# An attention and mixture-of-experts kernel: slot 0's list from one-hots of 168 places, and the gate's reciprocal taken in the expert slots

## The chip, the cores and the metric

The kernel runs on one core of one Trainium2 chip. The metric is the device time of one execution in microseconds (us); of the kernel before three executions were timed. The engines are TensorE (PE, with its weight loads as PEld), VectorE (DVE), ScalarE (ACT), GpSimd (POOL) and SyncE (SP, which here only issues transfers). ACT and POOL issue transfers too. Each engine runs its own fixed queue of instructions from first to last, and queues meet only at semaphores.

## The reference

Three layers run one behind the other: a causal attention (2 batches, 8 heads, 576 rows, 64 wide), then two mixtures of 8 experts over the 1152 rows of 512 that it leaves. What matters here is the first mixture:

```python
logits = x @ w_gate
expert_idx = np.argmax(logits, axis=1)
logits_s = logits - logits.max(-1, keepdims=True)
probs = np.exp(logits_s)
probs /= probs.sum(-1, keepdims=True) + 1e-09
gate_w = probs[np.arange(N), expert_idx]
for i in range(N):
    e = expert_idx[i]
    if counts[e] < capacity:
        disp[e, counts[e]] = x[i]; pos[i] = counts[e]; counts[e] += 1; keep[i] = True
h = np.maximum(np.einsum('ecd,edf->ecf', disp, w1), 0.0)
y = np.einsum('ecf,efd->ecd', h, w2)
for i in range(N):
    if keep[i]:
        out[i] = gate_w[i] * y[expert_idx[i], pos[i]]
```

The chosen expert's logit less the maximum is zero, so the gate is 1 / (sum of the exponentials + 1e-9). The second mixture is alike, with a bias by modality on the logits and no capacity.

## The kernel before

**Attention** goes by pairs of heads, four per batch. Its rows are written to a table x1 in HBM, 528 columns wide: 512 of the row, then column GATE (the gate), the token's number and the second mixture's biases. Rows lie on 128 partitions in NT = 5 tiles per batch.

**The door** is what this text calls the stretch between the last attention product and the first expert product, 97 to 109 us. For batch 1 `route` there takes the logits' maximum, the one-hot of the chosen expert (`oh1`), and by PE the counts of earlier rows with the same choice (`pr`); the exponentials' sum is taken by `gates`, which adds 1e-9, takes the reciprocal and puts it into x1's rows in SBUF (`xrow`, column GATE). Then four transfers write the last columns of batch 1 to x1 (`keep_rows`; the last one goes out on ACT's queue, row L268, the one before it on SP's, L269). Meanwhile `place` turns ranks into one-hots: a row's rank in its expert is split into a place inside a column of H1 = 96 (`here`, `lpos`) and the number of the column (`lcol` for all experts' columns, `lcol0` for the two columns of expert 0). PE multiplies them into lists of row numbers by `listing`: `pl0`, copied to `list0`, the rows of expert 0; and `pli`, copied to `list1`, those of all. Between these products, and behind them, PE runs products that nobody reads, to stay busy (`awake`; AWAKE gives their number at four places, the third of which, 14, stands right before slot 0's transposes).

**The slots.** Expert 0 is slot 0. Its rows come by two gathers of POOL (L828, reading x1 by `list0`) into the tile xc; PE transposes them (`ptx`, L869), ACT copies them (`xn`), and 128 products (L905) follow, first 64 into `ps`, in four groups j = 0 to 3 of 16. The PSUM pool of `ps` has two buffers, so group j = 2 can start only when both halves of group 0 have been read, one by ACT (L977) and one by DVE (L979, which is ordered behind ACT's). The experts after it run in an order of falling counts, `perm`, which DVE works out behind the lists (`key` to `perm`, L1206 to L1216). SP loads `perm` to know which expert's weights to fetch (L1122, then L146), POOL loads it to know which part of `list1` slot 1 gathers (L1118, then L1131 and L828). After a slot's first product come its tail's steps in `tail1`: the second mixture's logits, scaled by the row's gate, and its own gate times the first one's.

**What sets the order.** The order on each engine is made when the program is built, from the order of the code, pinned instructions (`keep_in_program_order`, `issue_after`) and a scheduler; `tail1`'s code before its first `yield` is in the program at the slot's beginning. On the chip each queue then runs as it stands.

Of the kernel before, what the change touches and what calls it, by code (L numbers as in the profile page):

```python
# [25 lines left out]
WHOLE = 72  # L26
RW = 528
# [19 lines left out]
AWAKE = 15, 6, 14, 4  # L47
# [7 lines left out]
def shape_constants():  # L55
# [9 lines left out]
    t = {"io8": np.broadcast_to(e - E, (NT, E)), "tok": tok, "tok1": tok1, "col": np.arange(E * J2),  # L65
# [27 lines left out]
def build(tc, ctx, spots, tab, qk, v, s, wg, wa, cap, mod, wg2, mb, wb, out):  # L93
# [42 lines left out]
    lcol0 = [ac.tile([P, NT, W1], F32R, name=f"lcol0{b}") for b in range(B)]  # L136
# [22 lines left out]
    def place(m, ge, rank, keep, pos, colm, num, p, nt, pool, colm0=None, rest=None, plain=None):  # L159
# [17 lines left out]
        def onehots():  # L177
            if keep is not None:
                here = pool.tile([p, shared, hc], F32R, name="here", bufs=1)
                shape = [p, shared, hc]  # L180
                order_ = []
                if plain is not None:
                    two = [p, nt, W[m]]
                    nc.vector.tensor_tensor(colm0, col[:p, 0:W[m]].unsqueeze(1).to_broadcast(two),
                                            hj.unsqueeze(2).to_broadcast(two), op=ALU.is_equal)
                    two = [p, shared, W[m]]
                    order_.append(nc.vector.tensor_tensor(colm0[:, 0:shared], colm0[:, 0:shared].bitcast(F32),
                                                          num[:, 0:shared].unsqueeze(2).to_broadcast(two),
                                                          op=ALU.mult).ins)
                    plain.append(here)  # L190
                with tc.issue_after(order_[0]) if order_ else ExitStack():
                    order_[1:] = [nc.vector.tensor_tensor(here, col[:p, 0:hc].unsqueeze(1).to_broadcast(shape),
                                            pb_[:, 0:shared].unsqueeze(2).to_broadcast(shape), op=ALU.is_equal).ins]
                for t in range(shared):
                    nc.scalar.mul(pos[:, t, :], here[:, t, :].bitcast(F32), num[:, t:t + 1])
            for t in range(shared, nt):
                with tc.issue_after(order_[-1]) if plain is not None else ExitStack():
                    last = nc.vector.tensor_scalar(pos[:, t, :], col[:p, 0:hc], pb_[:, t:t + 1], num[:, t:t + 1],
                                                   op0=ALU.is_equal, op1=ALU.mult)
            if colm0 is not None and plain is None:  # L200
# [3 lines left out]
            with tc.issue_after(last.ins):  # L204
                for t0, t1 in parts:
                    shape = [p, t1 - t0, 8 * nj]
                    def columns(t0=t0, t1=t1, shape=shape):
                        return nc.vector.tensor_tensor(colm[:, t0:t1],
                                                       col[:p, 0:8 * nj].unsqueeze(1).to_broadcast(shape),
                                                       hj[:, t0:t1].unsqueeze(2).to_broadcast(shape), op=ALU.is_equal)  # L210
                    if plain is not None and t0 == 0:
                        plain.append(columns)
                    else:
                        last = columns()
# [12 lines left out]
    with ExitStack() as actx:  # L227
# [44 lines left out]
        def route(b, behind_=None):  # L272
# [38 lines left out]
            nc.vector.tensor_tensor(rk, pr, oh1[b], op=ALU.mult)  # L311
# [4 lines left out]
            placing = lambda rest=None, plain=None: place(1, ge, rank, capf, lpos[b], lcol[b], tok1[:, b, :], P, NT, ap,  # L316
                                                          lcol0[b], rest, plain)
            if b:
                placing(plain=plain)
# [4 lines left out]
        postponed, plain = [], []  # L324
# [212 lines left out]
        def values(k):  # L537
# [15 lines left out]
            nc.vector.tensor_copy(k.xu[:, 320:576], pb)  # L553
# [56 lines left out]
        for n in range(2 * 2 * 4 + 1):  # L610
# [55 lines left out]
            if n == 7:  # L666
# [3 lines left out]
                with tc.issue_after(operands[-1]):  # L670
                    nc.gpsimd.tensor_copy(capf, capi[:, 0:1])
                    nc.gpsimd.tensor_copy(modf, modi[:, :, :, 0])
                for bb in range(B):
# [11 lines left out]
        with tc.issue_after(moved[0]):  # L685
            postponed.pop()()
# [14 lines left out]
        with tc.issue_after(counted.ins):  # L701
            awake(filler, ones, wide, AWAKE[1])
        pl0 = pst.tile([H1, W1], F32, tag="t", name="pl0")
        by_engine = [[0, 1, 2, 3, 4], [3, 4, 0, 1, 2]]
        in_line = [by_engine[0], by_engine[0]]

        def listing(dst, lc, b, between=False, turns=by_engine):
            for t in turns[b]:
                spot = plain[0] if b and t < 3 and turns is in_line else lpos[b]
                ins = nc.tensor.matmul(dst, spot[:, t, :], lc[b][:, t, :], start=(b == 0 and t == 0),  # L710
                                       stop=(b == 1 and t == turns[1][-1])).ins
# [788 lines left out]
```

## Time and profile before

| what | us |
|---|---|
| median of three executions | 391.19 |
| their lowest and highest | 391.06, 391.35 |
| the profiled execution's own time | 390.84 |
| its span | 389.1 |

The span is the time between the first and the last instruction of the profiled execution; 1.7 us of its time lie around it. Mean granted TensorE clock over the span is 0.988 of full speed. PE is busy for 97% of the span, DVE for 51%, ACT for 45%, POOL for 33%. Such shares are averages: the door is a small part of the span, and it is read from the timeline of each engine there. In a timeline row the first number is the start, the second the time that the row covers (several like instructions are one row, with their count behind the x), and in brackets stands the idle time before it and what released it.

### The profile page before, as it was taken

The page shows a single profiled execution, that of the slowest core. Times are in us where ns is not written, and L with a number is a line of the kernel's source. Part 1 is how long each engine was busy: PE and PEld are TensorE (multiplying, and loading weights), DVE is VectorE, ACT ScalarE, POOL GpSimd, SP SyncE. Part 2 cuts the span into 40 slices and gives each one's busy share as a digit, 9 for nine tenths or more (in the row PEclk, how much of TensorE's full clock was granted, in tenths as well). Part 3 has the DMA queues.
Part 4 walks back from the last instruction along what each step waited for, and adds up shares of the span by engine and source line. Part 5 has one row for each costly group of instructions (what it writes and reads, how often), then busy time and mean ns, then how long its engine had stood idle before and what let it go on. Part 6 is the DMA issues. An engine that isn't in the chain of part 4 may idle for free.

```text
span 389.1 us, 8687 instructions
## 1 busy us (share of the span) xinstructions
PE 376.5 (97%) x3058; PEld 353.6 (91%) x3058; DVE 198.6 (51%) x801; ACT 175.9 (45%) x473; POOL 126.8 (33%) x178
## 2 busy tenths in 40 slices
PE   7899999999999999999999999999999999999993
PEld 3788888888689999999999999999999999999992
DVE  6878889888826764251515161569722444221110
ACT  7999999996325632121221122155233464131120
POOL 4777877650270040421202002000425265020020
PEclk9699999999999999999999999999999999999998
DMA  5864699912159963969798779861287457010010
GB/s 189 289 196 161 238 373 380 322 72 93 55 177 290 353 192 95 322 201 320 234 319 236 258 210 291 280 217 36 61 310 292 123 168 219 5 39 21 0 56 25
DMA packets 29782, 75.08 MB, mean 193 GB/s; under 512 B 7547, under 2 KB 10859, under 8 KB 29728
## 3 DMA queue, kind: packets, MB, share of 16 engines
q1 hardware_dynamic: 27020, 67.19, 51.9%
q0 software_dynamic: 2624, 7.19, 6.4%
q8 instruction: 26, 0.43, 0.5%
q14 instruction: 28, 0.23, 0.2%
q10 hardware_dynamic: 84, 0.04, 0.0%
HBM read 63.97 MB, written 11.07 MB: 193 GB/s over the span
## 4 chain that ended last, share of the span: by engine, by line
PE 77%; issue 7%; DMA 6%; DVE 3%; POOL 3%; ACT 1%; SPq 1%; POOLq 1%; DVEq 0%; ACTq 0%
PE ps L905 30%; PE ps L913 7%; PE ps L914 7%; PE ps L915 7%; PE pt L423 5%; PE ps L423 4%; DMA qkd<-in_qk 4%; PE ps L909 3%; PE pb L423 2%; PE ptx L869 2%; PE pa L423 2%; DMA out<-yo,oi 2%; PE px L423 2%; PE pty L1001 1%; PE ps L911 1%
## 5 line engine op out<-in xcount | busy, mean ns | idle before, releaser
L905 PE MATMUL ps<-xn,st 128*128 128x160 f32 (+6 forms) x512 | 70.1, 290 | 0.3 <-ACT xn L890 0.3
L905 PEld LDWEIGHTS ps<-xn,st 128*128 128x128 f32 x512 | 66.2, 190 | 0.6 <-ACT xn L890 0.4
L905 PE MATMUL ps<-hidden,st 128*128 128x160 f32 (+5 forms) x448 | 62.4, 293 | 0.0
L905 PEld LDWEIGHTS ps<-hidden,st 128*128 128x128 f32 x448 | 58.5, 190 | 0.0
L513 ACT ACTIVATE e<-sc,nmx 128x192 f32<-128x192 f32 (+4 forms) x80 | 44.7, 561 | 1.6 <-DVE nmx L504 1.4
L971 DVE COPY yT<-ps 128x276 f32<-128x276 f32 (+6 forms) x22 | 8.0, 362 | 70.0 <-ACT yT L970 70.0
L913 PE MATMUL ps<-xs,hi 128*128 128x276 f32 x128 | 38.4, 300 | 0.0
L913 PE MATMUL ps<-hidden,hi 128*128 128x276 f32 x128 | 38.1, 298 | 0.0
L914 PE MATMUL ps<-xs,hi 128*128 128x276 f32 x128 | 37.1, 290 | 0.0
L915 PE MATMUL ps<-xs,lo 128*128 128x276 f32 x128 | 37.1, 290 | 0.0
L915 PE MATMUL ps<-hidden,lo 128*128 128x276 f32 x128 | 37.1, 290 | 0.0
L914 PE MATMUL ps<-hidden,hi 128*128 128x276 f32 x128 | 37.1, 290 | 0.0
L423 PE MATMUL pt<-ident,e 128*128 128x128 f32 x224 | 35.1, 288 | 0.5 <-ACT xu L552 0.4
L970 ACT COPY yT<-ps 128x276 f32<-128x276 f32 (+6 forms) x22 | 7.1, 323 | 60.6 <-PE ps L905 33.2
L423 PE MATMUL ps<-ka,qa 128*128 128x320 f32 (+2 forms) x96 | 31.0, 337 | 2.6 <-DVE nmx L504 1.4
L1092 POOL DMA_INDIRECT out<-yo,oi x13 | 12.4, 954 | 54.5 <-ACT yo L992 44.9
L803 DVE TENSOR_TENSOR lo<-st,hi 128x512 fp32r<-128x512 f32 x40 | 28.3, 730 | 1.1 <-ACT hi L801 1.0
L801 ACT CAST hi<-st 128x512 fp32r<-128x512 f32 x48 | 27.5, 620 | 0.0
L423 PEld LDWEIGHTS pt<-ident,e 128*128 128x128 f32 x224 | 25.9, 146 | 1.5 <-ACT xu L552 0.5
L828 POOL DMA_INDIRECT xc<-x,idx x14 | 13.9, 995 | 40.8 <-PE pr L1055 23.4
L984 DVE SCALAR_TENSOR_TENSOR hidden<-ps,hidden 128x552 fp32r<-128x552 f32 x16 | 11.7, 732 | 28.3 <-ACT hidden L982 28.2
L504 DVE CUSTOM_DVE_ANT_0 sc<-ps,later 128x192 f32<-128x192 f32 (+1 forms) x64 | 24.5, 413 | 2.7 <-PE ps L423 1.6
(317 smaller groups left out, 832.1 us busy)
## 6 DMA issues: line engine op xcount, KB each, us to landing
st<-in_wa SPq DMA_DIRECT2D x64, 512.0 KB
st<-in_wb SPq DMA_DIRECT2D x24, 512.0 KB
qkd<-in_qk SPq DMA_DIRECT2D x6, 1152.0 KB
vt<-in_v SPq DMA_DIRECT2D x8, 320.0 KB
qkd<-in_qk SPq DMA_DIRECT2D x4, 576.0 KB
out<-zrow SPq DMA_DIRECT2D x1, 2304.0 KB
y<-yt SPq DMA_DIRECT2D x8, 256.0 KB
x<-xrow SPq DMA_DIRECT2D x2, 768.0 KB
```

Of the source, the lines that this page charges most:

```text
L423: ins = op(*args, **kw)
L504: least[:] = [nc.vector.tensor_tensor_reduce(h.sc[t][:r, c0:c1], ps[:r, o0:o0 + c1 - c0], later[:r, m0:m0 + c1 - c0], -0.125, low, op0=ALU ...
L513: recent[:] = [nc.scalar.activation(to, h.sc[t][:r, :w], AF.Exp, bias=h.nmx[t][:r], scale=-1.0, accum_out=rsum[:r, k.b, t, n:n + 1]).ins]
L801: nc.scalar.copy(hi[:, c:c + h], st[:, c:c + h])
L803: eng.tensor_tensor(lo[:, c:c + h], st[:, c:c + h], hi[:, c:c + h].bitcast(F32), op=ALU.subtract)
L828: nc.gpsimd.indirect_dma_start(out=k.xc[:r, i, 0:rw], out_offset=None, in_=src, in_offset=bass.IndirectOffsetOnAxis(ap=idx[:r, i:i + 1], a ...
L905: pin(nc.tensor.matmul(out[:, 0:c], w[:, o:o + P], mv, start=first, stop=last, skip_group_check=True))
L913: pin(nc.tensor.matmul(out[:, 0:c], hi, mv[:, 0, :], start=first, stop=False, skip_group_check=True))
L914: pin(nc.tensor.matmul(out[:, 0:c], hi, mv[:, 1, :], start=False, stop=False, skip_group_check=True))
L915: pin(nc.tensor.matmul(out[:, 0:c], lo, mv[:, 0, :], start=False, stop=last, skip_group_check=True))
L984: fence(relu, nc.vector.scalar_tensor_tensor(k.hs[:, 2 * j:2 * j + 2, 1, :], k.b, 0.0, hi.bitcast(F32), op0=ALU.max, op1=ALU.subtract))
L1092: put = nc.gpsimd.indirect_dma_start(out=out, out_offset=bass.IndirectOffsetOnAxis(ap=oi[:, i:i + 1], axis=0), in_=yr[:, i, :], in_offset= ...
```

## The change

Slot 0's list for batch 1 no longer comes from places in a column times columns. For expert 0 the row's place in 168 is its count in `pr` itself, so DVE makes `r0` (the count, or a number out of range where another expert was chosen) and compares it with the numbers 0 to 167 (`col0`, made earlier on POOL, with places beyond the capacity moved out of range): `spots0`, in two instructions of 3 and 2 tiles. Ten products of one column pair each (`spots0` half by half, against a tile `tokr` with the token in one of two columns) add to `pl0`. The rest of `place` for batch 1 follows behind. `gates` only sums, straight into x1's column GATE; the 1e-9 and the reciprocal move to the beginning of `tail1`, once per slot, into `g1`, which the later steps read. AWAKE's second number falls from 6 to 3. The core of the diff:

```diff
+WHERE = 96 + WHOLE
-AWAKE = 15, 6, 14, 4
+AWAKE = 15, 3, 14, 4
             def gates():
-                g = ap.tile([P, NT], F32, name="g")
-                nc.vector.tensor_reduce(g, ex, axis=AX.X, op=ALU.add)
-                nc.vector.tensor_scalar_add(g, g, 1.0e-9)
-                return nc.vector.reciprocal(xrow[:, :, GATE], g).ins
+                return nc.vector.tensor_reduce(xrow[:, :, GATE], ex, axis=AX.X, op=ALU.add).ins
...
+            if b:
+                r0 = ap.tile([P, NT], F32, name="r0")
+                nc.vector.scalar_tensor_tensor(r0, oh1[1][:, :, 0], NONE, pr[:, :, 0], op0=ALU.mult, op1=ALU.add)
+                for t0, t1 in ((0, 3), (3, NT)):
+                    shape = [P, t1 - t0, WHERE]
+                    chosen = nc.vector.tensor_tensor(spots0[:, t0:t1, 0:WHERE], col0.unsqueeze(1).to_broadcast(shape),
+                                                     r0[:, t0:t1].unsqueeze(2).to_broadcast(shape), op=ALU.is_equal)
...
+                    nc.gpsimd.memset(tokr.bitcast(F32), 0.0)
+                    nc.gpsimd.memset(spots0[:, :, WHERE:C1].bitcast(F32), 0.0)
+                    nc.gpsimd.tensor_copy(tokr[:, :, 1], tok1[:, 1, :])
+                    nc.gpsimd.tensor_scalar(col0, col[:, 0:WHERE], capf, NONE, op0=ALU.is_ge, op1=ALU.mult)
...
-        first_list = listing(pl0, lcol0, 1, True, in_line)
+        for t in range(NT):
+            for i in (1, 0):
+                with tc.issue_after(ins):
+                    ins = nc.tensor.matmul(pl0, spots0[:, t, H1 * i:H1 * i + H1], tokr[:, t, 1 - i:3 - i], start=False,
+                                           stop=t == NT - 1 and i == 0).ins
         list0 = const.tile([H1, W1], I32, name="list0")
-        with tc.issue_after(listed(list0, pl0, 1).ins):
-            plain[1]()
-        with tc.issue_after(first_list):
-            placed = listing(pli, lcol, 1, True)
+        listed(list0, pl0, 1)
+        with tc.issue_after(ins):
+            placed = listing(pli, lcol[1], 1, [3, 4, 0, 1, 2], True)
...
     def tail1(k, c):
 
         k.yr, l8 = yrs[c % 2], l8s[c % 2]
+        g1 = mp.tile([H1, 2], F32, name="g1")
+        nc.vector.tensor_scalar_add(g1, k.xc[:, :, GATE], 1.0e-9)
+        nc.vector.reciprocal(g1, g1)
...
-            nc.vector.scalar_tensor_tensor(lg[:, i], lg[:, i], k.xc[:, i, GATE:GATE + 1], k.xc[:, i, BIAS:BIAS + E],
+            nc.vector.scalar_tensor_tensor(lg[:, i], lg[:, i], g1[:, i:i + 1], k.xc[:, i, BIAS:BIAS + E],
...
-        nc.vector.tensor_tensor(k.yr[:, :, GATE - DM], g, k.xc[:, :, GATE], op=ALU.mult)
+        nc.vector.tensor_tensor(k.yr[:, :, GATE - DM], g, g1, op=ALU.mult)
```

Three places in the queues move. On DVE, where the door's one-hots and lists are made, before (a name's number tells apart tiles of one name; 86 and 88 are batch 1's, 90 is `lcol0`'s; `list_1859` is `list0`):

```order
L174 SCALAR_TENSOR_TENSOR kept<-rank,capf,ctab 128x5
L166 TENSOR_REDUCE pb__1792<-ge 128x5
L168 TENSOR_REDUCE hj<-ge 128x5
L169 SCALAR_TENSOR_TENSOR pb__1792<-pb__1792,rank 128x5
L184 TENSOR_TENSOR lcol_90<-ctab,hj 128x10
L187 TENSOR_TENSOR lcol_90<-lcol_90,kept 128x6
L192 TENSOR_TENSOR here<-ctab,pb__1792 128x288
L198 TENSOR_SCALAR lpos_86<-ctab,pb__1792,kept 128x96 x2
L208 TENSOR_TENSOR lcol_88<-ctab,hj 128x208
L224 TENSOR_SCALAR list_1859<-pl_1839 96x2
L208 TENSOR_TENSOR lcol_88<-ctab,hj 128x312
```

After, first the new one-hots, and then the rest from `kept` on (`list_1862` is `list0`):

```order
L295 SCALAR_TENSOR_TENSOR r_1789<-oh_1_84,pr 128x5
L696 TENSOR_REDUCE cnt_1834<-pcnt 128x8
L298 TENSOR_TENSOR spots_90<-col_91,r_1789 128x3x168
L298 TENSOR_TENSOR spots_90<-col_91,r_1789 128x2x168
L302 TENSOR_TENSOR rk<-pr,oh_1_84 128x40
```

```order
L178 SCALAR_TENSOR_TENSOR kept<-rank,capf,ctab 128x5
L210 TENSOR_SCALAR list_1862<-pl_1841 96x2
L170 TENSOR_REDUCE pb__1798<-ge 128x5
L172 TENSOR_REDUCE hj<-ge 128x5
L173 SCALAR_TENSOR_TENSOR pb__1798<-pb__1798,rank 128x5
L185 TENSOR_TENSOR here<-ctab,pb__1798 128x288
L190 TENSOR_SCALAR lpos_86<-ctab,pb__1798,kept 128x96 x2
L199 TENSOR_TENSOR lcol_88<-ctab,hj 128x312
L199 TENSOR_TENSOR lcol_88<-ctab,hj 128x208
```

`spots0` and `list0` now stand ahead of `here`, `lpos` and both `lcol`, and of the two `lcol` the one of 208 elements, tiles 3 and 4, has become the last.

On PE, the products of the lists of batch 1 before (`pl_1839` is `pl0`, `pli` has the names 86 and 88 in it; L714 are the fillers between, L156 the first of the 14):

```order
L710 MATMUL pl_1839<-lcol_90,lpos_86 96x2
L710 MATMUL pli<-lcol_88,lpos_86 96x104
L714 LDWEIGHTS ones
L714 MATMUL ps<-ones 128x128
L710 MATMUL pli<-lcol_88,lpos_86 96x104
L714 LDWEIGHTS ones
L714 MATMUL ps<-ones 128x128
```

and after, from batch 0's products on:

```order
L705 MATMUL pli<-lcol_87,lpos_85 96x104 x5
L725 MATMUL pl_1841<-tokr,spots_90 96x2 x10
L705 MATMUL pli<-lcol_88,lpos_86 96x104
L709 LDWEIGHTS ones
L709 MATMUL ps<-ones 128x128
L705 MATMUL pli<-lcol_88,lpos_86 96x104
```

The five products of `pl0` with fillers between have become ten without; `pli`'s products, which start with tile 3, and then the 14 fillers follow as before.

On DVE behind the lists, before, around `perm` and then, eight rows on, ahead of `hidden` (`inv` belongs to slots 0 and 1, `hidden` to slot 0's first products):

```order
L1228 TENSOR_REDUCE wid<-eqw 128x7
L1216 TENSOR_TENSOR perm<-key,ctab 128x14
L1230 TENSOR_TENSOR more<-cnt_1829,wid 128x8
L1231 TENSOR_TENSOR more<-more,cnt_1829 128x8
L761 TENSOR_TENSOR s1cc<-more,ctab 128x48
L1010 TENSOR_SCALAR inv<-idx 96x2
```

```order
L774 TENSOR_TENSOR s1to<-s1ge,s1nxt 128x7x7
L778 TENSOR_REDUCE s1res<-s1ge 128x7
L777 TENSOR_REDUCE s1res<-s1to 128x7
L979 TENSOR_SCALAR hidden_1915<-ps 128x160 x3
L803 TENSOR_TENSOR lo<-st,hi 128x512
```

and after (`g_2198` is slot 0's `g1` from its rows `xc_710`, `g_2516` slot 1's from `xc_712`):

```order
L1229 TENSOR_REDUCE wid<-eqw 128x7
L1015 TENSOR_SCALAR g_2198<-xc_710 96x2
L1217 TENSOR_TENSOR perm<-key,ctab 128x14
L1231 TENSOR_TENSOR more<-cnt_1834,wid 128x8
L1016 RECIPROCAL g_2198<-g_2198 96x2
```

and, further on,

```order
L776 TENSOR_REDUCE s1res<-s1ge 128x7
L775 TENSOR_REDUCE s1res<-s1to 128x7
L1015 TENSOR_SCALAR g_2516<-xc_712 96x2
L1016 RECIPROCAL g_2516<-g_2516 96x2
L977 TENSOR_SCALAR hidden_1917<-ps 128x160 x3
L801 TENSOR_TENSOR lo<-st,hi 128x512
```

An instruction that reads slot 0's gathered rows now stands right ahead of `perm`, and two that read slot 1's stand right ahead of `hidden`.

## Rows read from the trace of the kernel before

**Rows 1.** By stretch: us, busy PE, PEld, DVE, ACT, POOL; PEclk, DMA, GB/s
```profile
97.00:104.00 7.00, 6.14 (x58) 4.69 (x57) 6.19 (x36) 3.30 (x14) 0.00 (x0) 1.00 0.16 47
109.00:127.00 18.00, 18.00 (x136) 18.00 (x137) 8.03 (x18) 6.93 (x18) 7.54 (x16) 1.00 0.81 259
350.00:373.00 23.00, 23.00 (x191) 23.00 (x190) 3.09 (x8) 4.16 (x10) 1.84 (x2) 1.00 0.04 12
```
**Rows 2.** Timeline (start us, us, what) of PE: fillers, transposes, slot 0's products
```profile
104.18 3.19 PE L156 MATMUL ps<-ones 128*128 128x512 bf16 x14
108.13 0.47 PE L869 MATMUL ptx<-ident,xc 72*128 72x72 f32 x4 [0.21 <-DMA xc<-x,list]
108.90 8.96 PE L905 MATMUL ps<-xn,st 128*128 128x160 f32 x64 [0.30 <-ACT xn L890]
```
**Rows 3.** POOL's queue at L828 (ns min/median/max, first, last start), then timeline
```profile
L828 POOLq EVENT_SEMAPHORE  x3: 43/43/214, 102.9 to 103.3; - x3
104.10 0.98 POOL L828 DMA_INDIRECT xc<-x,list  x1 [18.85 <-DVE s1to L773]
105.39 0.97 POOL L828 DMA_INDIRECT xc<-x,list  x1 [0.30 <-DVE wid L1228]
```
**Rows 4.** Timeline of the door, the last writes of x1 and their sources
```profile
99.49 0.50 ACT L589 ACTIVATE xrow<-ps,rinv 128x64 f32<-128x64 f32 x2
100.12 0.19 DVE L305 RECIPROCAL xrow<-g 128x5 f32<-128x5 f32 x1
100.48 0.51 ACTq L268 DMA_DIRECT2D x<-xrow  x1
```
**Rows 5.** Timeline of DVE, one-hots and lists of the door
```profile
100.37 0.20 DVE L311 TENSOR_TENSOR rk<-pr,oh 128x40 f32<-128x40 f32 x1
101.79 0.45 DVE L192 TENSOR_TENSOR here<-ctab,pb__1792 128x288 fp32r<-128x288 f32 x1
102.16 0.56 DVE L198 TENSOR_SCALAR lpos<-ctab,pb__1792,kept 128x96 fp32r<-128x96 f32 x2
102.64 0.37 DVE L208 TENSOR_TENSOR lcol<-ctab,hj 128x208 fp32r<-128x208 f32 x1
103.09 0.16 DVE L224 TENSOR_SCALAR list<-pl 96x2 int32<-96x2 f32 x1
103.17 0.47 DVE L208 TENSOR_TENSOR lcol<-ctab,hj 128x312 fp32r<-128x312 f32 x1
103.82 0.17 DVE L1206 SCALAR_TENSOR_TENSOR key<-cnt,ctab 128x7 f32<-128x7 f32 x1 [0.19 <-DVE lcol L208]
```
**Rows 6.** Timeline, `perm`, POOL's load of it and slot 1's gathers
```profile
105.28 0.17 DVE L1216 TENSOR_TENSOR perm<-key,ctab 128x14 int32<-128x14 f32 x1
L1118 POOLq TENSOR_LOAD <-perm x1: 498/498/498, 107.1 to 107.1; - x1
108.90 1.01 POOL L828 DMA_INDIRECT xc<-x,idx  x1 [0.59 <-POOL idx L1131]
110.22 0.96 POOL L828 DMA_INDIRECT xc<-x,idx  x1 [0.31 <-issue]
```
**Rows 7.** Transfers of the stretch 88 to 112, median us from issue to landing
```profile
xc<-x,list POOLq DMA_INDIRECT x2, 2.9
xc<-x,idx POOLq DMA_INDIRECT x2, 3.3
```
**Rows 8.** Waits of the same stretch (us in total, times, longest); then `hidden` on DVE
```profile
DVE inv L1010 <- POOL idx L1131: 2.1, 2, 1.2
111.77 0.32 DVE L979 TENSOR_SCALAR hidden<-ps 128x160 f32<-128x160 f32 x1 [2.38 <-ACT hidden L977]
```
**Rows 9.** Busy time by stretch again, where the granted clock fell early on
```profile
10.00:11.00 1.00, 0.00 (x0) 0.00 (x0) 0.99 (x4) 1.00 (x4) 0.00 (x0) 0.96 0.29 62
11.00:12.00 1.00, 0.61 (x1) 0.29 (x1) 0.94 (x5) 1.00 (x6) 0.00 (x0) 0.50 0.94 281
17.00:18.00 1.00, 1.00 (x7) 1.00 (x6) 0.86 (x4) 1.00 (x4) 0.91 (x7) 0.62 1.02 403
18.00:19.00 1.00, 1.00 (x10) 1.00 (x9) 0.91 (x5) 1.00 (x3) 0.95 (x1) 1.00 0.67 133
```

More of the change, by code (lines that the diff above doesn't have):

```diff
@@ L135, in build @@
     lcol = [ac.tile([P, NT, 8 * J1], F32R, name=f"lcol{b}") for b in range(B)]
-    lcol0 = [ac.tile([P, NT, W1], F32R, name=f"lcol0{b}") for b in range(B)]
+    lcol0 = ac.tile([P, NT, W1], F32R, name="lcola")
+    spots0 = ac.tile([P, NT, C1], F32R, name="spots0")
+    col0 = ac.tile([P, WHERE], F32, name="col0")
+    tokr = ac.tile([P, NT, 3], F32R, name="tokr")
     def fetch(src, e, i, pin=False):
@@ L157, in awake, with place @@
         return ins.ins
-    def place(m, ge, rank, keep, pos, colm, num, p, nt, pool, colm0=None, rest=None, plain=None):
+    def place(m, ge, rank, keep, pos, colm, num, p, nt, pool, colm0=None, rest=None):
         nj, hc, half = J[m], HC[m], con[f"half{m}"]
@@ L180, in onehots @@
                 shape = [p, shared, hc]
[L181 to L193, printed above, removed]
+                nc.vector.tensor_tensor(here, col[:p, 0:hc].unsqueeze(1).to_broadcast(shape),
+                                        pb_[:, 0:shared].unsqueeze(2).to_broadcast(shape), op=ALU.is_equal)
                 for t in range(shared):
@@ L196, in onehots @@
             for t in range(shared, nt):
[L197 to L200, printed above, removed]
+                last = nc.vector.tensor_scalar(pos[:, t, :], col[:p, 0:hc], pb_[:, t:t + 1], num[:, t:t + 1],
+                                               op0=ALU.is_equal, op1=ALU.mult)
+            if colm0 is not None:
                 shape = [p, nt, W[m]]
@@ L206, in onehots @@
                     shape = [p, t1 - t0, 8 * nj]
[L207 to L214, printed above, removed]
+                    last = nc.vector.tensor_tensor(colm[:, t0:t1], col[:p, 0:8 * nj].unsqueeze(1).to_broadcast(shape),
+                                                   hj[:, t0:t1].unsqueeze(2).to_broadcast(shape), op=ALU.is_equal)
             return last
@@ L315, in route @@
                 gates()
-            placing = lambda rest=None, plain=None: place(1, ge, rank, capf, lpos[b], lcol[b], tok1[:, b, :], P, NT, ap,
-                                                          lcol0[b], rest, plain)
+            placing = lambda rest=None: place(1, ge, rank, capf, lpos[b], lcol[b], tok1[:, b, :], P, NT, ap,
+                                              None if b else lcol0, rest)
             if b:
-                placing(plain=plain)
+                placing()
             else:
@@ L322, in route @@
             return exp
-        postponed, plain = [], []
+        postponed = []
         def load(p):
@@ L552, in values @@
             recent.append(nc.scalar.copy(k.xu[:, 0:320], pa).ins)
-            nc.vector.tensor_copy(k.xu[:, 320:576], pb)
+            with tc.issue_after(k.hold) if k.p == 7 else ExitStack():
+                nc.vector.tensor_copy(k.xu[:, 320:576], pb)
             k.rinv = ap.tile([P, NT, 2], F32, name="rinv")
@@ L685, in build @@
         with tc.issue_after(moved[0]):
-            postponed.pop()()
+            pairs[7].hold = postponed.pop()().ins
         values(pairs[7])
@@ L701, in build, with listing @@
         with tc.issue_after(counted.ins):
-            awake(filler, ones, wide, AWAKE[1])
+            last_fill2 = awake(filler, ones, wide, AWAKE[1])
         pl0 = pst.tile([H1, W1], F32, tag="t", name="pl0")
[L704 to L711, printed above, removed]
-                if between and t != turns[1][-1]:
+        def listing(dst, lc, b, turns, between=False):
+            for t in turns:
+                ins = nc.tensor.matmul(dst, lpos[b][:, t, :], lc[:, t, :], start=(b == 0 and t == 0),
+                                       stop=(b == 1 and t == turns[-1])).ins
+                if between and t != turns[-1]:
                     with tc.issue_after(ins):
```

13 lines of the change are left out of this document (8 added, 5 removed).

## The prediction

> **What bounds the kernel now.** I read the busy time by stretch first. From 109 us on PE is busy in every microsecond: 18.00 of 18 us at the first slots, 23.00 of 23 far into the second mixture, at a granted clock of 1.00 [rows 1]. So what delays PE's work behind the door is not made up later; it goes to the end in full, and nothing that DVE, ACT or POOL do beside it counts unless PE waits for it. In the door, 97 to 104 us, PE is busy for 6.14 of 7 us, but part of that is fillers [rows 1], so there the chain of waits counts.
>
> Backwards from the first product: L905 starts at 108.90, behind ACT's `xn`, behind transposes of which the second four, at 108.13, waited for a transfer, slot 0's second gather [rows 2]. That gather was issued at 105.39, 1.29 behind the first, at 104.10 [rows 3]. Before the first one POOL's queue sits in three waits, from 102.9 to 103.3 [rows 3], that end with the landing of x1's last writes, issued at 100.48 [rows 4]; from there it takes a fixed 0.8 or so to issue. `list0` is done at 103.09 + 0.16 = 103.25 [rows 5]. That too is within those waits' end, so I can't say from this alone that only the writes bind; both ends are priced below. The writes wait for the reciprocal, which ends at 100.31 [rows 4].
>
> A second chain runs beside it: `perm` on DVE at 105.28, POOL's load of it at 107.1, slot 1's gathers at 108.90 and 110.22 [rows 6], landed 3.3 us after issue [rows 7], at 113.5. Slot 1 needs its rows only when slot 0 is through, so this chain has much room now.
>
> **The change, part by part.**
>
> *The reciprocal leaves the rows.* Two small DVE steps go, and the sum is in x1's rows before 100.0. Then ACT's last copies into those rows bind the write: 99.49 + 0.50 = 99.99 [rows 4] in place of 100.31, with the same 0.17 to the issue. So the write, and with it the gathers, come 0.32 earlier: 103.78 and 105.07, the second landed 108.13 - 105.39 = 2.74 later, at 107.81 [rows 2, 3].
>
> *`list0` from 168 places.* r0 stands about where `rk` stood, 100.37 [rows 5]. The three `lcol`/`here` rows give the price of one-hots: 208 elements 0.37, 288 0.45, 312 0.47 [rows 5], about 0.96 ns an element and 0.17 fixed. So 504 take 0.66 and 336 take 0.49: `spots0` is done near 101.7. Ten products follow, of which four wait for the second half; today 0.37 lies between the end of `lpos`, 102.72, and the start of `list0`, with two products in it [rows 5], so four take about 0.7, and `list0` ends near 102.5, against 103.25. If the list binds the gather today, that is worth up to 0.75; if the writes bind, 0.32. I take 0.32, since x1's writes and not the list are what POOL's queue waited for longest (214 ns of a wait, the first of three) [rows 3].
>
> *The other lists come later.* The DVE order puts `spots0` and `list0` ahead of `pb_`, `here`, `lpos` and both `lcol`. Behind `list0` at 102.5 come three small steps at 0.13 (from `rk` to `here` eleven steps took 1.42) and then the same 0.45 to 0.56 us rows: `here` at 102.97 against 101.79 [rows 5], 1.2 late, and the last `lcol` ends near 104.6, where before it ended at 103.17 + 0.47 = 103.64. Its last piece is now tiles 3 and 4, with which `pli` starts, so all five products of `pli` come behind it; before, three came behind 103.64 and took until the fillers' start at 104.18 [rows 2], 0.18 each. Five take 0.9: the fillers start at 105.4 to 105.5. Fourteen took 3.19 [rows 2], so the transposes start at about 108.5 with both gathers landed, and L905 starts near 109.5. **PE starts slot 0 0.6 late**, though its rows are there 0.3 early. PE's idle stretch from 102.4 to 104.7 is new.
>
> *`g1` of slot 0 stands ahead of `perm` on DVE.* It reads gathered rows, so DVE stops there until 107.81. Without it `perm` would come with its chain, 0.96 late at 106.24 (behind `key`, which started at 103.82 once the last `lcol` was done [rows 5]); with it, at 108.0 to 108.1. DVE takes its queue in order: today's `inv` held it for up to 1.2 us in the same way [rows 8]. Behind `perm`, POOL's load starts at 108.2 instead of 107.1, and slot 1's gathers move by the same 1.08, to 109.98 and 111.30; with 3.3 to land [rows 6, 7] their rows are there at 114.60. SP's weight fetches also wait for `perm`, and come 1.3 later at least; the weights of slot 0 and the first of slot 1 are fetched long before, so I take nothing.
>
> *`g1` of slot 1 stands ahead of `hidden` on DVE.* Two instructions of the 0.17 to 0.19 size of such rows, and they wait for 114.60. So DVE reads slot 0's group 0 not at 111.77 [rows 8] but at about 114.9, and is done 0.32 later, 115.2. Group 2 of the products needs that buffer. It would have started at 108.90 + 8.96 / 2 = 113.38 [rows 2]. **PE stalls there and goes on at 115.25, 1.87 late.** The 0.6 of its later start lies inside this: groups 0 and 1 end at 114.0 and then wait 1.25.
>
> *All else.* `g1` costs two small DVE steps in each of eight slots, about 3 us in all, beside DVE's 8.03 of 18 busy [rows 1]; from slot 2 on the rows that they read are gathered a slot ahead. POOL makes `col0` and clears `spots0` during attention in its own pauses, and three fillers fewer take out time of which PE had it to spare. A few ACT copies move a place in attention. I bound all of this by -0.1 and +0.2 and take 0.
>
> **The sum.** On the profiled execution: 390.84 + 1.9 = 392.7. That execution lies 0.35 under the median of three, 391.19; on the median the sum is 391.19 + 1.9 = **393.1 us**. The open term is the landing of slot 1's gathers: 2.74, as slot 0's took, makes the shift 1.3 (392.5); each microsecond more, with weight fetches beside it (DMA 0.81 busy behind the door [rows 1]), adds one, and I allow half of one: 393.7. A list that binds takes a further 0.4 off, at most: 392.1.
>
> **Rivals.**
>
> *The clock falls.* Early in the run PE idles through the whole of 10 to 11 us, after weak microseconds, and the granted clock drops to 0.50, 1.2 GHz, for 11 to 17.7 us, though PE is busy again from 12 on [rows 9]. The new idle 2.3 us at 102.4, after a door with pauses, resembles it; against it, that idle is shorter than all the weak time before 11 us, and a ten-product burst and the fillers lie around it. If it falls at about 104.7 and stays for the same 6.7 us, fourteen fillers take twice 3.19, +3.2, and L905 starts near 112.9, 4.0 late; DVE's waits are then covered. That gives 391.19 + 4.0 = **395.2**; a fall only at the later 1.25 us stall costs up to 3.3 on top of 1.9, the same 396.
>
> The Trainium skill ("TensorE: Matmul & The Clock Gate", section "What's actually happening") says that throttled is the default and activity releases it, so three fillers fewer and ten bare products in the place of five with fillers between speak against this change; by that rule the time would be this rival's. The trace agrees that an idle PE lost its clock, at 10.9 us; no row shows a fall after a pause this short.
>
> *Not slower: the rows land in time.* If slot 1's rows landed by 112.9, DVE would serve group 0 before PE needs the buffer, and only the start of slot 0 would count: +0.6 for the fillers, **391.8**. That needs a landing 1.6 after the second gather's issue at 111.30, against 2.74 for the fastest in the rows, or `perm` not held at all. It decides at that point; below it the price is the fillers' alone.
>
> *Faster.* If the fillers didn't hold the transposes either (the last `lcol` by 103.9), the earlier writes remain: 390.84 to 390.9, and with a binding list 390.4. The queues as they stand speak against it twice.
>
> **How the numbers follow.** Forecast 0.60, the clock's fall 0.26, rows in time 0.10, faster path 0.04. The range holds the forecast with its bounds and the clock's fall: 392.1 to 395.3; some 0.15 is left out. About 0.2%, 0.8 us, is what a measurement of this kernel can tell from no change: faster 0.03, within it 0.11, slower 0.86.
>
> **What would show it.** In the changed kernel's trace: the write of x1 at about 100.16 and slot 0's gathers near 103.8 and 105.1; `list0` near 102.5; the fillers from about 105.4; L905 near 109.5; DVE idle from about 106 to 107.8 with slot 0's gathers as the releaser of `g`, `perm` at 108; a second idle time of DVE up to 114.6 before slot 1's `g`; a pause of PE of about 1.25 us between the second and third group of L905. A granted clock of 0.50 anywhere behind 104 would mean the first rival. Without a pause in L905 the forecast is wrong; with `perm` before 107 its first half is.

## The result, and the profile after

The changed kernel takes 395.89 us (median of 5, 395.37 to 396.11) against 391.18 for the kernel before (5 runs, 391.06 to 391.35): a ratio of 1.0119, 95% interval 1.0109 to 1.013. It is slower, as forecast, but by 4.7 us and not by 1.9; 393.1 was too low and the range, 392.1 to 395.3, doesn't hold it. The profiled execution took 395.45 with a span of 393.5, 4.4 more than before.

Where the 4.4 us lie is read best from PE, by how much later the same instruction starts than in the trace before: at the transposes of 72 us in attention 0.51 (0.10 of it stands there from 35 us on); at the first product of slot 0 2.70 (111.60 against 108.90, [rows 2]); at its third group of products 3.23 (116.58, where before it started at 113.35); at the products between 137 and 146 us, which are slot 1's, 4.01 and then 4.30; at the end 4.4. Behind 146 us next to nothing is added.

PE by stretch in the door and behind it, after (columns as in [rows 1]: us, busy PE, PEld, DVE, ACT, POOL, granted clock, DMA, GB/s):

```profile
97.00:104.00 7.00, 5.52 (x57) 4.48 (x53) 5.73 (x29) 2.42 (x12) 0.00 (x0) 1.00 0.16 47
104.00:109.00 5.00, 3.85 (x16) 2.13 (x17) 2.68 (x16) 0.87 (x3) 3.04 (x5) 0.66 0.22 55
109.00:113.00 4.00, 3.70 (x26) 2.73 (x25) 1.98 (x16) 0.88 (x4) 1.55 (x3) 1.00 0.02 6
113.00:118.00 5.00, 4.63 (x34) 4.39 (x33) 0.92 (x4) 0.61 (x2) 4.18 (x10) 1.00 0.77 204
118.00:127.00 9.00, 9.00 (x70) 9.00 (x69) 4.23 (x8) 4.17 (x10) 2.64 (x6) 1.00 0.87 275
```

The granted clock is 0.66 on average from 104 to 109, so for much of it at 1.2 GHz, where before it was 1.00 throughout; by single microseconds it is 0.71 from 105 to 106, 0.50 to 108 and 0.58 to 109. The timeline of PE there, after:

```profile
101.91 1.01 PE L725 MATMUL pl<-tokr,spots 128*96 128x2 f32 x10
105.14 0.29 PE L705 MATMUL pli<-lcol,lpos 128*96 128x104 f32 x1 [2.23 <-DVE lcol L199]
106.23 4.49 PE L160 MATMUL ps<-ones 128*128 128x512 bf16 x14
110.55 0.75 PE L867 MATMUL ptx<-ident,xc 96*128 96x96 f32 x8
111.60 4.61 PE L903 MATMUL ps<-xn,st 128*128 128x160 f32 x32 [0.30 <-ACT xn L888]
116.58 4.61 PE L903 MATMUL ps<-xn,st 128*128 128x160 f32 x32 [0.37 <-DVE hidden L977]
```

PE waits 2.23 us for the last `lcol`, as worked out; then the 14 fillers take 4.49 us instead of 3.19 [rows 2], and slot 0 starts behind them. After two groups comes the forecast pause for `hidden`, but of 0.37 us, not 1.25, since PE itself came late. DVE and POOL, timeline after:

```profile
102.95 0.16 DVE L210 TENSOR_SCALAR list<-pl 96x2 int32<-96x2 f32 x1
104.33 0.77 DVE L199 TENSOR_TENSOR lcol<-ctab,hj 128x312 fp32r<-128x312 f32 x2
109.07 0.17 DVE L1015 TENSOR_SCALAR g<-xc 96x2 f32<-96x2 f32 x1 [2.13 <-DMA xc<-x,list]
109.15 0.16 DVE L1217 TENSOR_TENSOR perm<-key,ctab 128x14 int32<-128x14 f32 x1
115.90 0.21 DVE L1015 TENSOR_SCALAR g<-xc 96x2 f32<-96x2 f32 x1 [4.08 <-DMA xc<-x,idx]
116.23 0.69 DVE L977 TENSOR_SCALAR hidden<-ps 128x160 f32<-128x160 f32 x2
```

```profile
104.35 1.60 POOL L826 DMA_INDIRECT xc<-x,list  x1 [18.54 <-DVE here L185]
106.25 1.00 POOL L826 DMA_INDIRECT xc<-x,list  x1 [0.30 <-DVE gt L1212]
111.34 1.01 POOL L826 DMA_INDIRECT xc<-x,idx  x1 [0.59 <-POOL idx L1132]
112.65 0.96 POOL L826 DMA_INDIRECT xc<-x,idx  x1 [0.30 <-issue]
```

Both waits of `g1` are there: DVE is idle 2.13 us ahead of `perm` for slot 0's rows and 4.08 us ahead of `hidden` for slot 1's. New against the prediction is the first gather of POOL: 1.60 us, where it took 0.98 [rows 3], while DVE runs `lpos` and `lcol` beside it. The second comes 1.90 behind it and not 1.29.

Two things I hadn't seen at all. In attention, timelines of DVE, POOL and PE after:

```profile
66.71 1.41 DVE L274 TENSOR_SCALAR ge<-mn 128x5 f32<-128x5 f32 x1
66.63 1.46 POOL L365 TENSOR_TENSOR kb<-qkd,ka 64x576 fp32r<-64x576 f32 x1 [0.38 <-ACT ka L363]
72.15 0.52 PE L414 MATMUL pt<-ident,e 128*128 128x128 f32 x3 [0.23 <-DVE rinv L547]
```

A DVE step on 128x5 numbers takes 1.41 us and ends with POOL's instruction beside it (66.71 + 1.41 = 68.12; 66.63 + 1.46 = 68.09), the product that makes the keys' operand `kb`. In the trace before the same two were

```profile
66.18 0.17 DVE L288 TENSOR_SCALAR ge<-mn 128x5 f32<-128x5 f32 x1
66.66 1.44 POOL L374 TENSOR_TENSOR kb<-qkd,ka 64x576 fp32r<-64x576 f32 x1 [0.92 <-ACT ka L372]
```

the DVE step was through before POOL began. POOL's `kb` starts at the same time in both traces; it is DVE's step that comes 0.53 later. What stands ahead of them, after:

```profile
65.33 0.20 DVE L288 TENSOR_REDUCE xrow<-ex 128x5 f32<-128x40 f32 x1 [0.48 <-ACT ex L286]
64.84 1.41 POOL L359 TENSOR_TENSOR qa<-qkd,qb 64x576 fp32r<-64x576 f32 x1
```

DVE's queue now has the gate's sum ahead of steps that stood ahead of it before, and waits 0.48 there for ACT's exponentials; and POOL, which made `col0` first, comes to its product for the queries, `qa`, 0.51 later (64.33 before).

And beside slot 1's products, after, DVE's rows, POOL's, and PE's:

```profile
139.21 2.45 DVE L1008 TENSOR_SCALAR inv<-idx 96x2 f32<-96x2 int32 x1
139.28 2.38 DVE L801 TENSOR_TENSOR lo<-st,hi 128x512 fp32r<-128x512 f32 x1
140.10 1.57 DVE L964 TENSOR_TENSOR b<-ps,b 128x384 f32<-128x384 f32 x1
138.43 1.48 POOL L826 DMA_INDIRECT xc<-x,idx  x1 [0.30 <-issue]
140.22 1.42 POOL L1283 MEMSET yc<- 96x1560 f32 x1
141.82 0.44 PE L907 MATMUL ps<-hidden,hi 128*128 128x384 f32 x1 [0.48 <-DVE b L964]
```

These DVE steps, which take 0.15 to 0.7 us elsewhere, all end at 141.66, with POOL's last memset (141.64); PE waits for one of them. Before, slot 3's gather waited for DVE, and the memset of `yc` came when these steps were done:

```profile
138.16 1.24 POOL L828 DMA_INDIRECT xc<-x,idx  x1 [1.51 <-DVE dd L1061]
140.98 1.42 POOL L1282 MEMSET yc<- 96x1560 f32 x1
```

After, PE is 3.3 us later here, and yet the memset of `yc` starts at 140.22 and the first of slot 3's two gathers at 136.03. They are earlier because the last step of slot 0's tail reads `g1` and no longer slot 0's gathered rows, so that their buffer is free sooner, and slot 3's gathers and the memsets behind them in POOL's queue go ahead (`g1_mid_fill9_read` below tests this).

### The profile page after: what moved, and what is told of

It reads as the page before. It is cut to its first block, busy times and chain, and to the rows that moved or that the text cites. A ratio compares the mean times of both kernels' runs of the same rounds, so it can differ in the third digit from the quotient of the medians.

```text
span 393.5 us, 8704 instructions
## 1 busy us (share of the span) xinstructions
PE 378.6 (96%) x3056; PEld 353.5 (90%) x3056; DVE 203.7 (52%) x814; ACT 176.1 (45%) x473; POOL 131.0 (33%) x184
## 4 chain that ended last, share of the span: by engine, by line
PE 58%; issue 7%; DMA 3%; DVE 3%; POOLq 1%; POOL 0%; ACT 0%; DVEq 0%
PE ps L903 28%; PE ps L911 7%; PE ps L912 7%; PE ps L913 7%; PE ptx L867 2%; DMA out<-yo,oi 2%; PE ps L907 2%; PE pty L999 1%; PE pty L989 1%; PE p L1021 1%; DMA xc<-x,idx 1%; DMA xc<-x,list 1%; PE ps L909 1%; DVE lo L801 1%; DVE inv L1008 1%
## 5 line engine op out<-in xcount | busy, mean ns | idle before, releaser
L826 POOL DMA_INDIRECT xc<-x,idx x14 | 15.3, 1092 | 59.9 <-DVE eq L1045 41.3
L801 DVE TENSOR_TENSOR lo<-st,hi 128x512 fp32r<-128x512 f32 x40 | 30.0, 772 | 1.5 <-ACT hi L799 1.4
L414 PE MATMUL ps<-kb,qb 128*128 128x320 f32 (+2 forms) x96 | 24.8, 304 | 1.4 <-POOL kb L365 0.5
```

The source lines that it names most:

```text
L414: ins = op(*args, **kw)
L801: eng.tensor_tensor(lo[:, c:c + h], st[:, c:c + h], hi[:, c:c + h].bitcast(F32), op=ALU.subtract)
L826: nc.gpsimd.indirect_dma_start(out=k.xc[:r, i, 0:rw], out_offset=None, in_=src, in_offset=bass.IndirectOffsetOnAxis(ap=idx[:r, i:i + 1], a ...
```

## The experiments

The theory tested (A): in the door two limits lie side by side, DVE held by `g1` (3.2 us) and the late lists with the halved clock (2.70 us; the expectations say 2.75), and each hides the other; attention and the stretch of slot 1 add their own. All kernels below start from the changed one unless said otherwise; each is compared with the kernel before on the same chip (390.9 to 391.1 there).

**g1 late, and nine fillers, alone and together.**

```diff
-        g1 = mp.tile([H1, 2], F32, name="g1")
-        nc.vector.tensor_scalar_add(g1, k.xc[:, :, GATE], 1.0e-9)
-        nc.vector.reciprocal(g1, g1)
...
         red = nc.vector.tensor_reduce(lg, ...)
+        g1 = mp.tile([H1, 2], F32, name="g1")
+        with tc.issue_after(red.ins):
+            nc.vector.tensor_scalar_add(g1, k.xc[:, :, GATE], 1.0e-9)
+        nc.vector.reciprocal(g1, g1)
```

> The changed kernel with g1's two DVE steps moved from the slot's start to right ahead of their first use. Theory A (two limits lie side by side in the door: DVE held by g1, which lets the third group of slot 0's products go on 3.2 us late, and the late lists with a halved clock, which start slot 0 2.75 us late): perm near 106.8, no pause in slot 0's products, slot 0 still starts near 111.6, and the time falls by only 0.4 to 0.6, to 395.2 to 395.5. Rival B (g1's wait alone carries the loss): the time falls by about 3, to 392 to 393.

Measured: 398.36 (397.66 to 400.8), ratio 1.0206 (1.0169 to 1.0243): slower than the changed kernel (395.89), which neither theory had. The pauses of DVE and PE in slot 0 are gone, but the clock is 0.51 in 104 to 109 and slot 0 starts at 112.87, and a new wait of PE comes in slot 0's tail:

```profile
143.01 0.17 PE L1054 MATMUL pr<-oh,upper 96*96 96x16 bf16 x1 [3.04 <-DVE lo L801]
```

Two steps more in the chain from `lg` to `oh` moved `oh` behind other work of DVE, and there into POOL's memsets (its row has 1.98 us, to 142.92). So this run tells of the clock and of POOL, but not what `g1` early costs.

```diff
         with tc.issue_after(ins):
+            ins = awake(filler, ones, wide, 9)
+        with tc.issue_after(ins):
             placed = listing(pli, lcol[1], 1, [3, 4, 0, 1, 2], True)
```

> The changed kernel with 9 more fillers of 512 columns behind slot 0's list products, where PE idled 2.2 us. Theory A: the granted clock stays at 1.00 from 104 to 109, slot 0 starts near 110.1, but the pause ahead of its third group grows to about 2 us and the time stays within 0.3 of 395.9. Rival C (the halved clock alone carries the loss): slot 0's earlier start goes to the end, 394.2 to 394.6.

Measured: 397.52 (396.33 to 400.17), ratio 1.0191 (1.0149 to 1.0233). The stretch and PE's timeline of this kernel:

```profile
104.00:109.00 5.00, 4.75 (x28) 2.45 (x27) 2.34 (x13) 0.90 (x3) 3.06 (x5) 1.00 0.20 55
110.08 4.62 PE L905 MATMUL ps<-xn,st 128*128 128x160 f32 x32 [0.30 <-ACT xn L890]
117.35 1.90 PE L905 MATMUL ps<-xn,st 128*128 128x160 f32 x12 [2.66 <-DVE hidden L979]
```

The clock stays at 1.00 and slot 0 starts at 110.08 as worked out, and nothing of it is kept: PE pauses 2.66 us for `hidden`. That is the two limits side by side. The time is worse than expected: here DVE's queue has six small steps between `g1` and `perm`, so `perm` comes at 109.84 and not at 109.15, and the runs above 398 have a mean clock of 0.982 and 0.990 against 0.998 for the two near 396.4; why theirs is lower no trace shows.

> Both edits together. Theory A: both limits are gone, slot 0 starts near 110.1 and runs through: 1.2 us late instead of 3.2, so 393.6 to 394.0 if the 1.1 us lost between 137 and 146 us stay, 392.5 if they go. If only one limit mattered, this is the same as the better one of the two single edits.

Measured: 396.33 (394.99 to 398.44), ratio 1.0149 (1.0109 to 1.0189): slot 0 starts at 110.41 and runs through, but PE waits 3.04 us again in slot 0's tail, for the longer chain (the same row, at 140.54). The time is 2.3 over what I expected, for the same reason as in the first.

**The list's part alone** (the gate as before: sum, 1e-9 and reciprocal in the rows, no `g1`).

> The changed kernel with the gate as before (sum, 1e-9 and reciprocal in the rows, no g1): the list's part alone. Theory A: no loss in attention at 72 us (0.5 less), the clock falls in the door as in the changed kernel, slot 0 starts 2.2 to 2.7 late without a later pause, the loss between 137 and 146 is not there since the slot's rows are read by the last step as before: 393.4 to 394.0. If the gate's part carried all, 391.2.

Measured: 394.57 (394.07 to 395.64), ratio 1.0101 (1.0082 to 1.0119), 0.6 over what I expected. The door is as expected (clock 0.77 from 104 to 109, no pause in slot 0's products, no loss between 137 and 146). But the loss in attention is there, and larger, 1.33 us at 72 us: DVE's `g` has 0.78 us at 65.64 and `eq` 0.96 at 67.29. So that loss doesn't need the gate's new place.

**The gate's part alone** (from the kernel before; the later steps of `tail1` read `g1`).

```diff
             def gates():
+                return nc.vector.tensor_reduce(xrow[:, :, GATE], ex, axis=AX.X, op=ALU.add).ins
...
     def tail1(k, c):
+        g1 = mp.tile([H1, 2], F32, name="g1")
+        nc.vector.tensor_scalar_add(g1, k.xc[:, :, GATE], 1.0e-9)
+        nc.vector.reciprocal(g1, g1)
```

> The kernel before with the gate's part alone: the sum into the rows, 1e-9 and reciprocal in the slots (g1 at the slot's start), lists as before. Theory A: the door's lists and fillers stay, so the clock stays at 1.00 and slot 0 starts within 0.6 of 108.9; slot 1's g1 ahead of hidden makes a pause of about 1 us before the third group; between 137 and 146 another 0.5 to 1.2 may go, since the slot's rows are freed earlier. 392.3 to 394. Rival (the gate's part is harmless, the lists carry all): 391.0 to 391.4.

Measured: 392.64 (392.59 to 392.93), ratio 1.0041 (1.0027 to 1.0056). PE's timeline:

```profile
108.42 4.61 PE L902 MATMUL ps<-xn,st 128*128 128x160 f32 x32 [0.30 <-ACT xn L887]
113.88 4.61 PE L902 MATMUL ps<-xn,st 128*128 128x160 f32 x32 [0.84 <-DVE hidden L976]
```

Slot 0 starts 0.48 early, the gain of the earlier write; the pause is 0.84; slot 1's loss is there (from 0.65 to 1.60 late between 127 and 143, with DVE's `inv` at 2.45 us again). Attention loses nothing.

**POOL's memsets moved behind.**

```diff
-        at(2, 5, lambda lst=lst: ...memset(lst, int(NONE)))
+        at(4, 5, lambda lst=lst: ...memset(lst, int(NONE)))
-        at(1 + i, 5, lambda i=i: clear(rings[2][i]))
+        at(1 + 3 * i, 5, lambda i=i: clear(rings[2][i]))
```

> The changed kernel with POOL's clearing of the second mixture's lists and of its second and third row buffers put two and more slots later. Theory A (POOL's memsets hold DVE's TENSOR_SCALAR on SBUF until they end): DVE's rows of 1.6 to 2.5 us near 140 shrink, PE's wait of 0.5 at 141.8 goes, 394.7 to 395.1 where the changed kernel has 395.9. Rival (the early gathers alone do it, or the weights): no change, 395.6 to 396.1.

Measured: 394.79 (394.69 to 395.01), ratio 1.0096 (1.0079 to 1.0113): 0.9 us less than the changed kernel by the two ratios (0.0023 of 391), whose intervals just touch. The gathers are as early as there (136.32 and 138.72), and DVE is free:

```profile
139.50 0.16 DVE L1008 TENSOR_SCALAR inv<-idx 96x2 f32<-96x2 int32 x1
139.57 0.68 DVE L801 TENSOR_TENSOR lo<-st,hi 128x512 fp32r<-128x512 f32 x1
```

From 127 us to the end this kernel adds next to nothing. So the memsets held DVE, not the gathers or the weights; `inv` now takes 0.16 us beside the second gather.

**Causes taken away one by one.** First `g1` behind the slot's `l8` copy, where the rows have long landed and no chain waits, 9 fillers, and batch 0's gate sum behind its one-hot:

```diff
+        l8c = nc.vector.tensor_copy(l8[:, 0:k.c], p8)
+        with tc.issue_after(l8c.ins):
+            nc.vector.tensor_scalar_add(g1, k.xc[:, :, GATE], 1.0e-9)
+        nc.vector.reciprocal(g1, g1)
...
             if not b:
+                with tc.issue_after(chose.ins):
                     gates()
```

> The changed kernel with g1 behind the slot's l8 copy, 9 fillers behind slot 0's list, and batch 0's gate sum behind its one-hot in DVE's queue. Theory A: no loss at 72 us, clock 1.00 in the door, slot 0 starts 0.6 to 0.7 late and runs through; what is left is that and up to 1.1 between 137 and 146: 391.6 to 392.8. If DVE's waits or the clock were not the cause, 395 or more.

Measured: 393.53 (393.35 to 393.68), ratio 1.0063 (1.0046 to 1.008). Clock 1.00, and PE in one piece:

```profile
110.19 8.96 PE L906 MATMUL ps<-xn,st 128*128 128x160 f32 x64 [0.30 <-ACT xn L891]
```

That is 1.3 late, of which 0.74 stands there at 72 us: the loss in attention stayed, so the gate sum's place isn't all of its cause (the time is 0.7 over the upper end of what I expected). Its way is another here. DVE no longer waits for ACT, but POOL's late `qa` holds the step before:

```profile
65.70 0.75 DVE L268 SCALAR_TENSOR_TENSOR eq<-d,ctab 128x40 f32<-128x40 f32 x1
64.98 1.42 POOL L360 TENSOR_TENSOR qa<-qkd,qb 64x576 fp32r<-64x576 f32 x1
```

and the step on 128x5 comes at 66.83, beside `kb` again, with 1.41 us. Slot 1's loss is there, 0.8.

Then one step more, which reads the gathered rows late and so frees them as late as before:

```diff
+        with tc.issue_after(inverse.ins):
+            nc.vector.scalar_tensor_tensor(g1, k.xc[:, :, GATE], 0.0, g1, op0=ALU.mult, op1=ALU.add)
         nc.vector.tensor_tensor(k.yr[:, :, GATE - DM], g, g1, op=ALU.mult)
```

> The same with one more small DVE step per slot, which reads the gate in the slot's rows right before the tail's last product, so that the rows are freed as late as before the change. Theory A: slot 3's gathers go back behind that step, and the loss between 137 and 146 goes: 391.5 to 392.0. Rival: the loss there comes from elsewhere, and the time is that of the kernel without this step.

Measured: 392.23 (392.02 to 392.82), ratio 1.0032 (1.0023 to 1.0042): slot 1's loss is gone, and slot 3's first gather is back behind the tail's steps, at 139.03. The time is 0.2 over what I expected.

Then `g1` behind the copy as the only edit:

> The changed kernel with g1 behind the slot's l8 copy and nothing else: the clock's limit without DVE's. Theory A: no pause in slot 0's products, slot 0 starts 2.7 to 4 late by how long the clock stays at 0.50, and DVE is still held near 137 to 141: 394.6 to 396.3, so little or nothing is gained on the changed kernel. Rival (g1's wait alone): 392.5 to 393.2.

Measured: 395.24 (394.84 to 395.54), ratio 1.0106 (1.0091 to 1.0122). No pause in slot 0, but it starts at 112.09, behind 14 fillers of 4.88 us, with the clock at 0.75 from 104 to 109. With DVE's limit away, the clock's carries nearly all: some 0.5 us is gained, by the ratios, and their intervals overlap. With the fillers alone nothing was gained, with both (`g1_mid_fill9`) 2.2, 1.0063 against 1.0119.

And POOL's six new instructions (`col0`, `tokr`, the clearing) behind its last attention work, that is behind the loop over heads and no longer inside it, as the only edit:

```diff
+        with tc.issue_after(operands[-1]):
+            nc.gpsimd.memset(tokr.bitcast(F32), 0.0)
...
```

> The changed kernel with POOL's six new instructions moved behind its last attention work (86 to 89 us) and nothing else. Theory A: POOL's product of batch 0's last keys starts earlier again and DVE's row of 1.41 us at 66.7 goes or shrinks, as long as that step comes before 66.65: up to 0.5 less in attention, 395.3 to 395.9. If the gate sum's place in DVE's queue alone was the cause, no change at 72 us.

Measured: 395.07 (394.81 to 395.72), ratio 1.0106 (1.0091 to 1.0122), 0.2 below what I expected. The loss at 72 us is gone (71.94 against 71.91 before); DVE and POOL there:

```profile
66.19 0.17 DVE L274 TENSOR_SCALAR ge<-mn 128x5 f32<-128x5 f32 x1
66.69 1.45 POOL L365 TENSOR_TENSOR kb<-qkd,ka 64x576 fp32r<-64x576 f32 x1 [0.94 <-ACT ka L363]
```

`kb` is where it was, `qa` is back at 64.34, and in the DVE queue of this build the gate's sum stands behind `eq` again, so this edit alone took away both ways into the loss. That POOL's six instructions are its cause follows from the next kernel too: it differs from `g1_mid_fill9_read` at this point by their place alone, with the gate's sum pinned in both, and between 67 and 72 us it loses 0.06 where that one loses 0.57. Only 0.3 of the span is gained, since the clock stays at 1.2 GHz longer here and slot 0 starts 2.89 late.

**The changed list with all of this, and the gate's part with all of this.** The first also takes the other lists' products in the order 0 to 4.

> The changed kernel with all causes taken away as far as they can be: g1 behind the l8 copy, 9 fillers behind slot 0's list, batch 0's gate sum behind its one-hot, the late reading step, POOL's six new instructions moved behind its last attention work, and the products of the other lists in the order 0 to 4, so that only two of them wait for the last column one-hots. Theory A: no loss at 72 us (0.7 less than without the POOL move), slot 0 starts 0.3 to 0.5 late, behind POOL's second gather, which the first still holds up: 391.2 to 391.7. If the loss at 72 were not POOL's work, 392.

Measured: 392.03 (391.84 to 392.84), ratio 1.0028 (1.0016 to 1.004), a little more than expected. POOL and PE:

```profile
104.02 1.78 POOL L830 DMA_INDIRECT xc<-x,list  x1 [15.47 <-DVE here L185]
106.11 1.00 POOL L830 DMA_INDIRECT xc<-x,list  x1 [0.30 <-DVE nth L1218]
109.25 0.47 PE L871 MATMUL ptx<-ident,xc 72*128 72x72 f32 x4 [0.28 <-DMA xc<-x,list]
```

With fillers and clock out of the way, slot 0 waits for its second gather, 0.72 late against [rows 3], since the first one takes 1.78 us beside DVE's one-hots for the other lists. That price belongs to the list's new place: in all eleven kernels with the new list the first gather takes 1.3 to 1.8, and in the three with the old lists 0.98.

The second has the old lists, the gate's sum in the rows, `g1` behind the copy, and the late reading step.

> The kernel before with the gate's part alone, but g1 behind the slot's l8 copy, and one small DVE step per slot that reads the gate in the slot's rows right before the tail's last product. Theory A: the earlier write of x1 stays (slot 0 starts 0.48 early, as in the gate's part alone), there is no pause in slot 0's products and no frozen DVE near 137: 390.4 to 390.6 against 390.95 to 391.18 of before, faster than both kernels. Rival: the early start is lost again to something later, within 0.2 of before.

Measured: 390.57 (390.33 to 391.21, 11 runs) against 391.05 (17 runs), ratio 0.9992, interval 0.9982 to 1.0001. PE's timeline:

```profile
108.49 5.70 PE L902 MATMUL ps<-xn,st 128*128 128x160 f32 x40 [0.30 <-ACT xn L887]
```

Slot 0 starts 0.41 early, and nothing takes it back; the span is 388.7 against 389.1. The median is 0.5 lower, but the interval just touches no change: it is the lowest median here, and that it is faster than the kernel before isn't shown.

## Why the prediction was wrong

Step by step, with the 0.53 us by which the door begins later (the one-hot `oh` at 100.34 against 99.81) taken off each time:

*The reciprocal leaves the rows: right.* The first gather comes at 104.35 - 0.53 = 103.82 (forecast 103.78). `gates_only` keeps the gain at PE, 0.48. (The write itself was issued at 100.48.)

*`list0` and the other lists: right in size.* `list0` starts at 102.42 and ends 0.16 later (forecast end 102.5), the last `lcol` ends at 104.57 (104.6), PE's idle stretch is 2.23 (2.3). `gates_only`, with the old `list0`, has its first gather 0.36 early: the writes bound the gather, as taken, and not the list.

*What the fillers cost: wrong, by the clock.* I took 3.19 us for 14 fillers at 1.00; they took 4.49, and 4.2 to 5.3 in the other kernels without the nine fillers. The clock's fall was my rival at 0.26, and it happened: in all six traces with this idle stretch the granted clock from 104 to 109 was 0.50 to 0.77; in all five with the stretch filled it was 1.00, and in the two with the old lists and the new gate too. The Trainium skill ("TensorE: Matmul & The Clock Gate", section "What's actually happening") says that throttled is the default and that activity releases it; the traces agree, since activity put back into the stretch kept the clock. The rival's price was too high, 4.0 for the door against 2.19 (2.70 less the 0.51 of attention) here, since the clock was down for some 3.4 us (a mean of 0.66 over 5 us) and not 6.7; in `g1_late` and `pool_moved` it was down for 6.8, and slot 0 started 4.0 and 2.9 late. The price that the prediction gives for a fall at the later pause is mis-added: 1.9 and 3.3 on 391.19 are 396.4, not the same as 395.2, and the range doesn't hold it.

*`g1` ahead of `perm`, and ahead of `hidden`: right as mechanisms, late by one term.* Both waits are in the trace, and `fill9` shows that they bind by themselves. My 1.87 became 3.23: 0.51 came from attention; 0.61 from the second gather, whose issue I took at 1.29 behind the first and which came at 1.90; 0.24 is the rest, most of it that POOL took up `perm` 0.26 behind its end instead of at once. 1.87 + 0.51 + 0.61 + 0.24 = 3.23. SP's loads of `perm` would by the same sum be 2.8 later and not 1.3; they start at 109.5 where they started at 105.6, and PE waits for no weights, as I took it.

So rival and forecast were both at work, and hid each other: 2.70 and 3.23, of which the larger counts. That is why neither edit alone gave back more than some 0.5.

*"All else", bounded by -0.1 and +0.2: the step that failed.* I took it at 0, and it held 0.51 in attention and 1.07 from slot 0's third group of products to 146 us, 1.6 of the 4.4. "POOL makes `col0` ... in its own pauses" was wrong as a reason: the pauses are POOL's, but DVE and POOL hold each other up, and with the six instructions there a DVE step of 0.17 us fell beside POOL's product of keys and took 1.41. "From slot 2 on the rows that they read are gathered a slot ahead" was true and looked at the wrong side: I asked when `g1` could read, not when the rows' buffer became free, and what POOL would then start sooner. The same coupling is in the 0.61 of the gather. The sum of what I had not counted, 0.51 + 0.61 + 0.24 + 1.07 + 0.1 behind 146 us, is 2.5, and 1.9 + 2.5 is the 4.4 of the spans.

The range failed with it: its upper end was the clock's rival alone, with nothing for two effects at once.

## What to carry to other kernels

An instruction that reads gathered rows, put at the head of a slot's program, stands in a queue in front of work that has nothing to do with them: look at what is behind it, and force it down if need be. When a path has two limits of nearly the same length, undoing one shows little; undo both before a cause is dismissed. And work that is moved on DVE or POOL is to be checked against what the other one does in the same microsecond, also where a buffer that comes free earlier lets POOL start earlier.

## What the runs showed of the hardware

Some DVE steps between tiles in SBUF stand still while POOL works, and all that is behind them in DVE's queue stands with them. A `TENSOR_SCALAR` on 128x5 took 1.41 us instead of 0.17 beside POOL's product, and one on 96x2 2.45 us: it began 0.69 ahead of the first memset's row, beside a gather, and ended with the third memset, without being let in between; with the memsets gone it took 0.16 beside the same gather. POOL's gathers took 1.60, 1.78 and 2.09 us beside busy stretches of DVE, instead of 0.96 to 1.0; that DVE holds them is read from the overlap, since no run took DVE's steps away. The Trainium skill ("SBUF — State Buffer", section "Who interferes with whom") says that the two share a pair of ports, and that against DVE in its two-port modes, which `tensor_scalar` can enter, the one that issues first has the pair for the whole instruction while the other is blocked; the traces agree for the first step, which began 0.08 behind POOL's product, and add that steps on 5 and 2 columns are held too. For the second step POOL's rows don't show which of the two came first. Not every pair collides: in the trace before, a `TENSOR_TENSOR` of DVE ran beside a POOL memset at its usual speed:

```profile
116.57 0.69 DVE L803 TENSOR_TENSOR lo<-st,hi 128x512 fp32r<-128x512 f32 x1 [0.18 <-ACT hi L801]
115.97 1.42 POOL L1282 MEMSET yc<- 96x1560 f32 x1
```

The clock fell around an idle stretch of PE of 2.2 us, but not at one point of it: in `pool_moved` it was 1.00 from 101 to 102, 0.77 from 102 to 103 and 0.50 behind that, with PE idle from 102.42 on; in `list_only`, with PE idle from 103.74 to 105.97, it was still 1.00 from 105 to 106 and 0.85 from 106 to 107. What is shown is that nine fillers in the stretch keep the clock at 1.00, in five traces of five. How much of the fall is the pause and how much the thinner work ahead of it (three fillers fewer, ten products without fillers between) no run separates. It stayed at 1.2 GHz for 3.4 us in four of the six traces and for 6.8 in two, `g1_late` and `pool_moved` (fillers of 4.2 to 5.3 us); from what, stays open.
